# Turned order of the block products in each batch's first pair, 13 instead of 24 loads of w versions, and a new instruction order

## The chip, the cores and the metric

The kernel runs on one core of a Trainium2 chip, as one launch. The metric is device time in microseconds. Three runs of the kernel before gave 339.51, 339.52 and 339.85 us, so its median is 339.52 us. A separate, profiled execution took 343.12 us.

## The reference

Inputs are q, k, v (4 batches, 4 heads, 1088 positions, 32 channels), S1 and S2 (8 x 32), and the weights of a gated layer. Everything is float32.

```
phi(x)  = outer product of (S1 x) and (S2 x), 64 features per position and head
x       = (phi(q) . sum_s phi(k) v) / (phi(q) . sum_s phi(k) + 1e-6)      # [4, 1088, 128]
h       = gelu(x @ w_in)                                                 # d_ff = 1024
u, v    = h[..., :512], h[..., 512:]
v_n     = (v - mean) / sqrt(var + 1e-6) * g_ln
v_s     = einsum('ts,bsd->btd', w_sg, v_n) + b_sg[t]                     # 1088 x 1088 per batch
out     = x + (u * v_s) @ w_out
```

The large product is `w_sg` (called w here) with v_n, once per batch. Most of the work is in it.

## The kernel before, in words

**Precision.** Operands are split in two words, a high one and a low one (`w_h`, `w_l`; the two halves of `ar` for v_n), and a product is three matmuls: high x high, low x high, high x low. These are lines 832, 833 and 834, in `group`.

**Tiling.** The 1088 columns of w (positions t) are three thirds of 362, 362 and 364 columns (`CH`). The 1088 rows are eight tiles of 128 and a last one of 64. The 512 channels of v_n are four blocks of 128. A block of channels times a third of w over all rows is a `whole`: eight groups and a `tail` (lines 843, 844). Results gather in two PSUM banks, `pz0` and `pz1`, which `pair` calls X and Z.

**Seven products instead of eight.** In batches 1 to 3, two blocks of channels (A1 and A2) make a pair, with two pairs in a batch. The first two thirds of w, cut into rows 0 to 511 and 512 to 1023, are treated as a 2 x 2 block matrix, and a pair takes seven block products (`product`, four groups each) of sums of blocks, in place of eight, and two wholes for the third third (results `ca` and `cb`). Sums and differences of v_n blocks are made by VectorE into `tmp` (called `sg`) and into v_n's own place, and split by `words` or `split` into four buffers `ar`; `e` says which buffer a product reads. `evac` (line 763, VectorE) moves a result out of its bank with scale and bias; `unit` makes u (lines 747 to 749), `gate` multiplies the two and adds the product with w_out (lines 784 to 786).

**Versions of w's middle third.** The products need sums of w's blocks. `combine` makes them once, during batch 0, in eight halves one after another: each loads pieces of w into `tmp` (line 880), works on VectorE and ScalarE, and stores the results to a DRAM tensor `td` (lines 897 to 899). One set (`t4`) stays on chip. Four others are in DRAM: "1" and "2" for rows 0 to 511 (half 0), "3" and "b" for rows 512 to 1023 (half 4); "b" is the original. `stream(n, half)` loads one of them over the middle third of `w_h` and `w_l`: two transfers of 362 KB (line 904) and four of 181 KB (line 906), each after the last matmul that reads what it overwrites. `product(..., (0, 1), ...)` and `product(..., (4, 1), ...)` read the streamed versions of half 0 and half 4; `(0, 0)` and `(4, 0)` read the first third, which never changes, and "t4" the set on chip.

**How a pair goes.** In the kernel before each of the six pairs loads all four versions. Its first product of a streamed version comes after one product and a whole. Loads of a pair: "1" after its third product, "b" after its fifth, "2" and "3" further on. Two more loads (lines 1224 and 1225) come ahead of the first pair. The last pair skips "2" and "3".

**Order.** Each operation is a task with a number, given in the order of the program text, and `ORDER` (line 42) lists all 2038 tasks in the order in which they are issued. Each engine, and the queue on SyncE that issues the DMAs, takes its own tasks in that order. Attention of batch b+1 (lines 909 on) is interleaved with the pairs of batch b. Twelve matmuls called `keep` (line 695) compute nothing that is used. At the start, normalisation of batch 0 leads by VectorE (lines 289 to 304, 652, 660) to the first matmuls of w (line 683).

Of the kernel before, what the change touches and what calls it, by code (L numbers as in the profile page):

```python
# [19 lines left out]
NT = 9  # L20
# [174 lines left out]
def tile_kernel(ctx: ExitStack, tc: tile.TileContext, qd, kd, vd, sd, wd, bd, wind, gd, woutd, identd, outd):  # L195
# [142 lines left out]
    g = Gate(0, xs[0])  # L338
# [702 lines left out]
    def pair(b, p, e, zi):  # L1041
# [52 lines left out]
        if more:  # L1094
            stream("2", 0)
# [7 lines left out]
        if more:  # L1103
            stream("3", 4)
# [193 lines left out]
```

## Time and profile before

| | us |
|---|---|
| median of 3 runs | 339.52 |
| profiled execution | 343.12 |
| its span, first to last instruction | 341.3 |
| TensorE matmul (PE) busy | 331.2 |
| TensorE weight loads (PEld) busy | 321.3 |
| VectorE (DVE) busy | 267.0 |
| ScalarE (ACT) busy | 217.9 |
| moved by DMA | 68.87 MB |

Busy times are of one engine over the whole span. Matmuls overlap in the records: a matmul of 362 columns has a row of 0.33 us, but the next starts 0.165 us after it. So the pace is read from the distance of two starts, and not from a row's duration.

### The profile page before, as it was taken

The page shows a single profiled execution, that of the slowest core. Times are in us where ns is not written, and L with a number is a line of the kernel's source. Part 1 is how long each engine was busy: PE and PEld are TensorE (multiplying, and loading weights), DVE is VectorE, ACT ScalarE, POOL GpSimd, SP SyncE. Part 2 cuts the span into 40 slices and gives each one's busy share as a digit, 9 for nine tenths or more (in the row PEclk, how much of TensorE's full clock was granted, in tenths as well). Part 3 has the DMA queues.
Part 4 walks back from the last instruction along what each step waited for, and adds up shares of the span by engine and source line. Part 5 has one row for each costly group of instructions (what it writes and reads, how often), then busy time and mean ns, then how long its engine had stood idle before and what let it go on. Part 6 is the DMA issues. An engine that isn't in the chain of part 4 may idle for free.

```text
span 341.3 us, 5976 instructions
## 1 busy us (share of the span) xinstructions
PE 331.2 (97%) x2000; PEld 321.3 (94%) x2000; DVE 267.0 (78%) x603; ACT 217.9 (64%) x533; POOL 53.1 (16%) x123
## 2 busy tenths in 40 slices
PE   8999999999999999979999999999999999999995
PEld 7996899999999999979999999999989999999994
DVE  3699889999987598858987488988775696767683
ACT  7478882475998976525688895663798873332331
POOL 2595681000004030000000240000003300000000
PEclk9999999999999999989999999999999999999999
DMA  7969554685656476993958855862939474974901
GB/s 236 388 228 346 178 152 106 214 238 129 176 160 181 128 230 180 293 297 100 292 185 268 251 174 187 235 187 82 285 115 314 136 241 120 271 250 131 293 29 67
DMA packets 56175, 68.87 MB, mean 202 GB/s; under 512 B 5008, under 2 KB 53456, under 8 KB 56144
## 3 DMA queue, kind: packets, MB, share of 16 engines
q1 hardware_dynamic: 56000, 68.40, 65.5%
q8 instruction: 16, 0.26, 0.3%
q14 instruction: 15, 0.12, 0.1%
q10 hardware_dynamic: 144, 0.09, 0.1%
HBM read 59.48 MB, written 8.99 MB: 201 GB/s over the span
## 4 chain that ended last, share of the span: by engine, by line
PE 81%; DMA 6%; DVE 6%; ACT 3%; SPq 1%; issue 1%; POOL 0%; DVEq 0%; ACTq 0%
PE pz L832 15%; PE pz L834 15%; PE pz L833 15%; PE ps L930 3%; DMA w_h<-td 2%; PE ps L747 2%; PE ps L748 2%; PE ps L749 2%; PE pz L844 2%; PE pz L843 2%; PE po L786 2%; PE po L785 2%; PE po L784 2%; PE ps L1012 2%; PE ps L1013 2%; PE ps L1014 2%
## 5 line engine op out<-in xcount | busy, mean ns | idle before, releaser
L832 PE MATMUL pz<-w_h,ar 128*128 128x362 f32 (+1 forms) x288 | 96.5, 335 | 2.2 <-DMA w_h<-td 2.2
L834 PE MATMUL pz<-w_l,ar 128*128 128x362 f32 (+1 forms) x288 | 95.3, 331 | 0.0
L833 PE MATMUL pz<-w_h,ar 128*128 128x362 f32 (+1 forms) x288 | 95.1, 330 | 0.0
L832 PEld LDWEIGHTS pz<-w_h,ar 128*128 128x128 f32 x288 | 54.7, 190 | 3.2 <-issue 2.5
L833 PEld LDWEIGHTS pz<-w_h,ar 128*128 128x128 f32 x288 | 54.7, 190 | 0.4
L834 PEld LDWEIGHTS pz<-w_l,ar 128*128 128x128 f32 x288 | 54.6, 190 | 0.3 <-DMA w_l<-td 0.3
L778 ACT CAST gh<-gt 128x362 fp32r<-128x362 f32 (+1 forms) x47 | 22.9, 493 | 24.1 <-PE po L785 12.8
L807 ACT CAST ar<-vn 128x512 fp32r<-128x512 f32 x40 | 24.5, 618 | 20.2 <-PE pz L834 19.4
L309 POOL TENSOR_TENSOR st<-st 128x4 f32<-128x4 f32 (+2 forms) x8 | 2.9, 366 | 190.2 <-DVE st L291 190.2
L779 DVE TENSOR_TENSOR gl<-gt,gh 128x362 fp32r<-128x362 f32 (+1 forms) x47 | 24.6, 529 | 7.9 <-ACT gh L778 7.8
L808 DVE TENSOR_TENSOR ar<-vn,ar 128x512 fp32r<-128x512 f32 x40 | 27.1, 684 | 3.4 <-ACT ar L807 3.1
L753 ACT ACTIVATE u<-ps 128x362 f32<-128x362 f32 (+1 forms) x48 | 21.8, 468 | 9.3 <-PE ps L749 5.9
L326 ACT ACTIVATE vn<-vn,st 128x512 f32<-128x512 f32 x33 | 25.8, 812 | 0.8 <-POOL st L320 0.8
L777 DVE TENSOR_TENSOR gt<-gt,u 128x362 f32<-128x362 f32 (+1 forms) x47 | 24.6, 529 | 0.6
L763 DVE SCALAR_TENSOR_TENSOR gt<-pz,g_col,b_bc 128x362 f32<-128x362 f32 (+1 forms) x31 | 18.3, 590 | 7.5 <-PE pz L834 3.6
L701 POOL TENSOR_TENSOR w_l<-w_f,w_h 128x362 fp32r<-128x362 f32 (+1 forms) x21 | 21.7, 1061 | 5.0 <-ACT w_h L654 4.1
L1021 ACT ACTIVATE vn<-ps 128x512 f32<-128x512 f32 x27 | 16.0, 594 | 5.8 <-PE ps L1014 5.7
L1024 ACT ACTIVATE kp<-vn,st 128x512 bf16<-128x512 f32 x27 | 19.4, 719 | 0.3
L747 PE MATMUL ps<-x_h,win_h 128*128 128x362 f32 (+1 forms) x48 | 15.9, 332 | 0.4 <-ACT ab L958 0.4
L263 DVE TENSOR_TENSOR kp<-ps,kb 128x256 f32<-128x256 f32 x27 | 11.0, 417 | 6.3 <-ACT kb L925 4.5
L784 PE MATMUL po<-gh,wout_h 128*128 128x362 f32 (+1 forms) x47 | 15.8, 337 | 0.0
L748 PE MATMUL ps<-x_h,win_l 128*128 128x362 f32 (+1 forms) x48 | 15.8, 328 | 0.0
(300 smaller groups left out, 813.7 us busy)
## 6 DMA issues: line engine op xcount, KB each, us to landing
w_h<-td SPq DMA_DIRECT2D x48, 362.0 KB
w_l<-td SPq DMA_DIRECT2D x96, 181.0 KB
w_f<-in_w SPq DMA_DIRECT2D x9, 544.0 KB
tmp<-in_w SPq DMA_DIRECT2D x16, 181.0 KB
vx<-in_v SPq DMA_DIRECT2D x8, 288.0 KB
ea<-dq SPq DMA_DIRECT2D x12, 182.0 KB
eb<-dq SPq DMA_DIRECT2D x12, 182.0 KB
td<-tmp SPq DMA_DIRECT2D x8, 271.5 KB
```

The costliest lines, as they stand in the source:

```text
L326: A.activation(self.vn(t), self.vn(t), AF.Identity, bias=self.nm[:, t : t + 1], scale=self.rs[:, t : t + 1])
L747: mm(o, lhsT=win_h[:, ws], rhs=xh[:, cs], start=True, stop=False)
L748: mm(o, lhsT=win_l[:, ws], rhs=xh[:, cs], start=False, stop=False)
L777: add("V", dv(cw), lambda: V.tensor_mul(gt(k)[:, :cw], gt(k)[:, :cw], utt[plan.got[u]][:, :cw]), r=[u], w=[k], free=[u], port=1)
L778: add("A", ac(cw), lambda: A.copy(ght[plan.got[h]][:, :cw], gt(k)[:, :cw]), r=[k], take={h: "gh"})
L779: add("V", dv(cw), lambda: V.tensor_sub(glt[plan.got[l]][:, :cw], gt(k)[:, :cw], f32(ght[plan.got[h]][:, :cw])), r=[h, k], take={l: "gl"}, ...
L784: mm(o, lhsT=wout_h[:, db], rhs=hh, start=i == 1, stop=False, skip_group_check=True)
L807: add("A", ac(n), lambda: A.copy(dst[:, 0], q()), r=r, w=[key])
L808: add("V", dv(n), lambda: V.tensor_sub(dst[:, 1], q(), f32(dst[:, 0])), r=r, w=[key], port=1)
L832: mm(o, lhsT=ar[e][:, 0, t], rhs=wh, start=first, stop=False, skip_group_check=True)
L833: mm(o, lhsT=ar[e][:, 1, t], rhs=wh, start=False, stop=False, skip_group_check=True)
L834: mm(o, lhsT=ar[e][:, 0, t], rhs=wl, start=False, stop=last, skip_group_check=True)
```

## The change

The first pair of each batch (`turn`) takes its products in another order, and the second pair's order is changed a little, so that each pair ends with the versions of half 0 and half 4 that the next one starts with. A first pair uses "1" and "b" and then loads "2" and "3"; a second pair uses "2" and "3" and then loads "1" and "b". That makes two loads per pair, and one ("1") ahead of the first pair: 13 loads in place of 24. Number and shape of the matmuls, of the splits and of VectorE's sums stay as they were. In batch 1 the first pair's first product now reads "1", which is loaded just ahead of it. `ORDER` is a new list of 1972 tasks (66 fewer: 11 loads of six transfers). Three waits (`after=`) are added to the list's own dependencies; they constrain the list and add no instruction.

```diff
-        kw["after"] = gone(b)
+        kw["after"] = [*gone(b), ids["b"], ids["g"], *([ids["ng"]] if col is ng_col else [])]
-            add("PE", 0.222, k1, ..., after=[ids["pv0", NT - 1]] * (b == 1))
+            add("PE", 0.222, k1, ..., after=[ids["pv0", NT - 1], ids["skl"]])
-    def pair(b, p, e, zi):
+    def pair(b, p, e, zi, turn):
...
+        if turn:
+            add_(sg, a[1, 0], a[1, 1], ak[1, 0] + ak[1, 1], gk)
+            words(ar[e[0]], lambda: sg, ("ar", e[0]), gk)
+            split(b, A1, 0, e[1])
+            split(b, A1, 1, e[2])
...
+        if turn:
+            unit(b, ca)
+            product(Z, zk, e[0], (0, 1), True, (1, 1))
+            stream("2", 0)
+            words(ar[e[0]], lambda: sg, ("ar", e[0]), gk)
+            evac(b, c22, Z, zk, g_col)
+            whole(X, xk, 2, (e[1], e[2]), 0)
+            evac(b, ca, X, xk, g_col)
+            gate(b, ca)
+            unit(b, c12)
+            product(Z, zk, e[3], (4, 1), False, (1, 3))
+            stream("3", 4)
+            words(ar[e[3]], lambda: a[0, 0], ("ar", e[3]), ak[0, 0])
+            evac(b, c12, Z, zk, ng_col)
+            unit(b, c11)
+            product(X, xk, e[1], (0, 0), True)
+            split(b, A2, 1, e[1])
+            evac(b, c11, X, xk, g_col)
+            product(Z, zk, e[2], (4, 0), True, (0, 0))
+            split(b, A2, 0, e[2])
+            evac(b, c11, Z, zk, g_col, ("gt", b, c11), False)
+            gate(b, c11)
+            product(X, xk, e[0], (0, 1), False)
+            evac(b, c12, X, xk, g_col, ("gt", b, c12), False)
+            gate(b, c12)
+            unit(b, c22)
+            product(X, xk, e[3], (4, 1), False)
+            evac(b, c22, X, xk, ng_col, ("gt", b, c22), False)
+            gate(b, c22)
+            unit(b, cb)
+            whole(Z, zk, 2, (e[2], e[1]), 1)
+            evac(b, cb, Z, zk, g_col)
+            gate(b, cb)
+            unit(b, c21)
+            product(X, xk, e[1], "t4", False, (0, 2))
+            evac(b, c21, X, xk, ng_col)
+            gate(b, c21)
+            return
+
+        unit(b, c11)
         product(X, xk, e[0], (0, 0), True)
         evac(b, c11, X, xk, g_col)
-        whole(Z, zk, 2, e, 0)
...
+        product(Z, zk, e[1], (4, 0), True, (0, 0))
+        evac(b, c11, Z, zk, g_col, ("gt", b, c11), False)
+        gate(b, c11)
         product(X, xk, e[2], (0, 1), False)
         stream("1", 0)
         split(b, A2, 1, e[2])
         evac(b, c12, X, xk, g_col)
-        product(Z, zk, e[1], (4, 0), True, (0, 0))
+        unit(b, ca)
+        whole(Z, zk, 2, e, 0)
...
         product(X, xk, e[3], (4, 1), False)
         stream("b", 4)
...
         product(Z, zk, e[0], (0, 1), True, (1, 1))
-        if more:
-            stream("2", 0)
...
         product(Z, zk, e[1], (4, 1), False, (1, 3))
-        if more:
-            stream("3", 4)
...
         if ci == 1:
-            stream("2", 0)
-            stream("3", 4)
-    zi, e = 0, (2, 3, 0, 1)
+            stream("1", 0)
+    zi, e = 1, (2, 3, 0, 1)
...
-        pair(b, 0, e, zi)
+        pair(b, 0, e, zi, True)
...
-        pair(b, 1, e, 1 - zi)
+        zi, e = 1 - zi, (e[0], e[3], e[2], e[1])
+        pair(b, 1, e, zi, False)
+        e = (e[0], e[1], e[3], e[2])
```

Up to the first load (task 771) both lists number the tasks alike, so places can be compared. The last stores of `combine` (tasks 717 to 719) stand at places 905 to 917 in the old list and at 860 to 870 in the new one. Of the loads ahead of the first pair, the last transfer of 362 KB (task 774) stands at place 919 in the old list and 896 in the new one; the four groups of the first product that reads it stand at 937 to 944 (tasks 864 to 867) in the old list and at 899 to 924 (tasks 835 to 838) in the new one. The load of k of batch 1 for attention, and its first matmuls (line 922), come after the last `keep` in the new list, and among them in the old one. In batch 1, five groups of the whole on Z stand in the new list between the sixth product of the first pair and the seventh, which use the same bank X.

## Rows read from the trace of the kernel before

**Rows 1.** The page's first part: busy us, share and instructions of each engine.
```profile
PE 331.2 (97%) x2000; PEld 321.3 (94%) x2000; DVE 267.0 (78%) x603; ACT 217.9 (64%) x533; POOL 53.1 (16%) x123
```
**Rows 2.** Stretches of 8 us: busy us and instructions, TensorE's granted clock, DMA.
```profile
core 0: us, PE busy (x) PEld busy (x) DVE busy (x) ACT busy (x) POOL busy (x), PEclk, DMA share, GB/s
24.00:32.00 8.00, 7.98 (x44) 6.29 (x44) 7.20 (x28) 5.71 (x10) 4.64 (x6) 1.00 0.97 342
32.00:40.00 8.00, 7.27 (x43) 6.18 (x41) 7.14 (x20) 6.93 (x24) 6.09 (x16) 1.00 0.80 261
40.00:48.00 8.00, 7.43 (x50) 7.11 (x50) 7.60 (x21) 6.76 (x16) 6.20 (x15) 1.00 0.42 101
64.00:72.00 8.00, 7.58 (x46) 7.28 (x45) 7.32 (x16) 4.53 (x10) 0.00 (x0) 1.00 0.71 185
136.00:144.00 8.00, 8.00 (x48) 7.49 (x47) 6.75 (x14) 4.42 (x9) 0.00 (x0) 1.00 0.92 273
144.00:152.00 8.00, 5.79 (x31) 5.52 (x30) 4.37 (x10) 2.30 (x5) 0.00 (x0) 0.89 1.03 311
152.00:160.00 8.00, 8.00 (x45) 8.00 (x44) 6.48 (x12) 3.81 (x8) 0.00 (x0) 0.89 0.42 120
248.00:256.00 8.00, 7.78 (x43) 7.08 (x42) 5.92 (x14) 7.34 (x24) 0.00 (x0) 1.00 0.34 99
336.00:344.00 8.00, 1.40 (x6) 0.60 (x4) 1.45 (x5) 0.00 (x0) 0.00 (x0) 0.88 0.07 23
```
**Rows 3.** Waits of PE: line waited for, us in total, times, longest.
```profile
PE pz L832 <- DMA w_h<-td: 2.2, 1, 2.2
PE ps L922 <- DMA vn<-in_k: 0.7, 1, 0.7
PE ps L747 <- ACT ab L958: 0.4, 1, 0.4
PE ps L953 <- DVE kp L263: 0.3, 1, 0.3
PE ps L922 <- DVE kp L263: 0.3, 1, 0.3
PE ps L1012 <- ACT vn L1021: 0.2, 1, 0.2
```
**Rows 4.** Timeline 138 to 160: start us, us, engine, line, instruction, idle before.
```profile
138.67 0.33 PE L832 MATMUL pz<-w_h,ar 128*128 128x362 f32 x1
...
140.65 0.19 PEld L834 LDWEIGHTS pz<-w_l,ar 128*128 128x128 f32 x1 [0.28 <-DMA w_l<-td]
...
143.00 0.19 PEld L832 LDWEIGHTS pz<-w_h,ar 128*128 128x128 f32 x1 [0.23 <-DMA w_h<-td]
...
146.78 0.33 PE L833 MATMUL pz<-t4b,ar 128*128 128x362 f32 x1
...
146.95 0.33 PE L834 MATMUL pz<-t4b,ar 128*128 128x362 f32 x1
...
149.48 0.41 PE L832 MATMUL pz<-w_h,ar 128*128 128x362 f32 x1 [2.21 <-DMA w_h<-td]
...
150.44 0.50 PE L832 MATMUL pz<-w_h,ar 128*128 128x362 f32 x1
...
153.74 0.33 PE L832 MATMUL pz<-w_h,ar 128*128 128x364 f32 x1
```
**Rows 5.** The chain that ended last, in order of time: start us, us, what.
```profile
141.22 8.13 DMA w_h<-td
```
**Rows 6.** Timeline of the DMA queue on SyncE, 128 to 152.
```profile
132.06 0.38 SPq L897 DMA_DIRECT2D td<-tmp  x1
...
134.85 0.43 SPq L904 DMA_DIRECT2D w_h<-td  x1
136.77 0.80 SPq L906 DMA_DIRECT2D w_l<-td  x2
```
**Rows 7.** DMA issues by kind, with count and KB of each.
```profile
w_h<-td SPq DMA_DIRECT2D x48, 362.0 KB
w_l<-td SPq DMA_DIRECT2D x96, 181.0 KB
```
**Rows 8.** Groups of VectorE instructions, the results moved out of a bank.
```profile
L763 DVE SCALAR_TENSOR_TENSOR gt<-pz,ng_col,gt 128x362 f32<-128x362 f32 x6 | 3.5, 591 | 2.3 <-PE pz L844 2.2
```

More of the change, by code (lines that the diff above doesn't have):

```diff
@@ L922, in k1 @@
                 mm(ps(pk)[:, :P], lhsT=vn[:, t, 256 * s : 256 * s + P], rhs=sk, start=True, stop=True)
-            add("PE", 0.222, k1, r=[("vn", s, t, 0)], take={pk: "ps"}, tune=at(b, "k", t), after=[ids["pv0", NT - 1]] * (b == 1))
+            add("PE", 0.222, k1, r=[("vn", s, t, 0)], take={pk: "ps"}, tune=at(b, "k", t), after=[ids["pv0", NT - 1], ids["skl"]])
             add("A", 0.09, lambda t=t, pk=pk: A.copy(kbt[t % 2], ps(pk)[:, 32:64]), r=[pk], w=[("kb", t % 2)])
@@ L955, in q2 @@
                 mm(o, lhsT=sk_h, rhs=ql, start=False, stop=True)
-            add("PE", 3 * pe(cw), q2, r=["qh", "ql"], take={pab: "ps"}, tune=at(b, "q", ci), after=[ids["pv0", NT - 1]] * (b == 1))
+            add("PE", 3 * pe(cw), q2, r=["qh", "ql"], take={pab: "ps"}, tune=at(b, "q", ci), after=[ids["pv0", NT - 1], ids["skl"]])
             add("A", ap(cw), lambda cw=cw, pab=pab: A.copy(abt[:, :cw], ps(pab)[:64, :cw]), r=[pab], w=["ab"], free=[pab])
@@ L1051, in pair @@
         end = b == B - 1 and p == 1
-        more = not end
         def both(i, src, r):
@@ L1056, in both @@
             add("V", dv(256), port=1, f=lambda: V.tensor_sub(rs[64:, i : i + 2], src[64:], f32(rs[64:, i : i + 2])), r=r, w=[("rs", i), ("rs", i + 1)])
-        split(b, A1, 0, e[0])
-        split(b, A1, 1, e[1])
-        both(0, vn[:, 8, 256 * s : 256 * s + 256].rearrange("p (t d) -> p t d", d=P), ak[0, 2] + ak[1, 2])
-        add("V", dv(512), port=1, f=lambda: V.tensor_add(a[0, 0], a[0, 0], a[1, 0]), r=ak[1, 0], w=ak[0, 0])
-        add("V", dv(512), port=1, f=lambda: V.tensor_add(sg, a[0, 0], a[1, 1]), r=ak[0, 0] + ak[1, 1], w=gk)
-        words(ar[e[2]], lambda: sg, ("ar", e[2]), gk)
-        words(ar[e[3]], lambda: a[0, 0], ("ar", e[3]), ak[0, 0])
+        add_ = lambda out, x, y, r, w: add("V", dv(512), port=1, f=lambda: V.tensor_add(out, x, y), r=r, w=w)
+        if turn:
[3 more added lines that the diff above has]
+            split(b, A1, 1, e[2])
+        else:
+            split(b, A1, 0, e[0])
+            split(b, A1, 1, e[1])
+        both(0, vn[:, 8, 256 * s : 256 * s + 256].rearrange("p (t d) -> p t d", d=P), ak[0, 2] + ak[1, 2])
+        add_(a[0, 0], a[0, 0], a[1, 0], ak[1, 0], ak[0, 0])
+        add_(sg, a[0, 0], a[1, 1], ak[0, 0] + ak[1, 1], gk)
+        if not turn:
+            words(ar[e[2]], lambda: sg, ("ar", e[2]), gk)
+            words(ar[e[3]], lambda: a[0, 0], ("ar", e[3]), ak[0, 0])
         add("V", dv(512), port=1, f=lambda: V.scalar_tensor_tensor(a[0, 1], sg, -1.0, a[0, 1], op0=ALU.mult, op1=ALU.subtract), r=gk, w=ak[0, 1])
-        add("V", dv(512), port=1, f=lambda: V.tensor_add(sg, a[1, 0], a[1, 1]), r=ak[1, 0] + ak[1, 1], w=gk)
+        if turn:
+            words(ar[e[3]], lambda: a[0, 1], ("ar", e[3]), ak[0, 1])
+        else:
+            add_(sg, a[1, 0], a[1, 1], ak[1, 0] + ak[1, 1], gk)
         add("V", dv(P), port=1, f=lambda: V.tensor_scalar(raw[:, 0], a[1, 2], -1.0, None, op0=ALU.mult), r=ak[1, 2], w=rk)
@@ L1069, in pair @@
         both(2, raw, rk)
-        unit(b, ca)
+        if turn:
+            unit(b, ca)
[9 more added lines that the diff above has]
+            stream("3", 4)
+            words(ar[e[3]], lambda: a[0, 0], ("ar", e[3]), ak[0, 0])
+            evac(b, c12, Z, zk, ng_col)
[24 more added lines that the diff above has]
+        unit(b, c11)
         product(X, xk, e[0], (0, 0), True)
         evac(b, c11, X, xk, g_col)
-        whole(Z, zk, 2, e, 0)
-        evac(b, ca, Z, zk, g_col)
-        gate(b, ca)
-        words(ar[e[0]], lambda: sg, ("ar", e[0]), gk)
-        unit(b, c11)
+        product(Z, zk, e[1], (4, 0), True, (0, 0))
+        evac(b, c11, Z, zk, g_col, ("gt", b, c11), False)
+        gate(b, c11)
         product(X, xk, e[2], (0, 1), False)
@@ L1082, in pair @@
         evac(b, c12, X, xk, g_col)
-        product(Z, zk, e[1], (4, 0), True, (0, 0))
+        unit(b, ca)
+        whole(Z, zk, 2, e, 0)
+        words(ar[e[0]], lambda: sg, ("ar", e[0]), gk)
         words(ar[e[1]], lambda: a[0, 1], ("ar", e[1]), ak[0, 1])
-        evac(b, c11, Z, zk, g_col, ("gt", b, c11), False)
-        gate(b, c11)
-        unit(b, c22)
+        evac(b, ca, Z, zk, g_col)
+        gate(b, ca)
         product(X, xk, e[3], (4, 1), False)
@@ L1091, in pair @@
         evac(b, c22, X, xk, ng_col)
-        unit(b, c21)
+        unit(b, c22)
         product(Z, zk, e[0], (0, 1), True, (1, 1))
-        if more:
-            stream("2", 0)
         evac(b, c22, Z, zk, g_col, ("gt", b, c22), False)
         gate(b, c22)
-        unit(b, c12)
+        unit(b, c21)
         product(X, xk, e[2], "t4", False, (0, 2))
@@ L1101, in pair @@
         gate(b, c21)
+        unit(b, c12)
         product(Z, zk, e[1], (4, 1), False, (1, 3))
-        if more:
-            stream("3", 4)
         evac(b, c12, Z, zk, ng_col, ("gt", b, c12), False)
@@ L1162, in standard @@
         gate(b, (db, ci))
-    add("A", 0.1, lambda: A.mul(ng_col, g_col, -1.0), w=["ng"], after=[ids["g"]])
+    ids["ng"] = add("A", 0.1, lambda: A.mul(ng_col, g_col, -1.0), w=["ng"], after=[ids["g"]])
     def new_swaps():
```

168 rows, old and new, of the table ORDER are left out of this document.

## The prediction

> **What bounds the kernel now.** First the page's busy times: PE is busy 331.2 us of a span of 341.3 us, DVE 267.0, ACT 217.9 [rows 1]. The change keeps all 2000 matmuls, so it can only work on the 10.1 us in which PE is not busy, and on matmuls that run slow. Next the table by stretches says where those 10.1 us lie: 0.73 us in 32 to 40, 0.57 in 40 to 48, 0.42 in 64 to 72, 2.21 in 144 to 152, 0.22 in 248 to 256, and 3.9 at the end, where 1.40 of the last 5.3 us are busy [rows 2]. The end is the last additions and stores, which the change leaves alone. So 144 to 152 is the stretch to look at: PE does 31 matmuls there against 48 in the stretch before, DMA is at a share of 1.03, and this stretch and the next show a granted clock of 0.89 on average where the others show 1.00 [rows 2]. PE's waits name the cause, 2.2 us in line 832 for a transfer of `w_h` from `td`, once [rows 3]. The chain that ended last holds that transfer: issued at 141.22, it took 8.13 us [rows 5]. It belongs to version "1" of the first pair of batch 1.
>
> A rule of the Trainium skill gives another size of the room. Perfetto Trace Analysis, section Identifying the Most-Contended Engine, says that matmul busy time judges TensorE badly and that the busy share of weight loads is to be taken; by that 341.3 - 321.3 = 20.0 us would be open [rows 1], twice as much. The stretch 24 to 32 speaks against it here: weight loads are busy 6.29 us of 8 while PE is busy 7.98 [rows 2], so there a weight load idles behind wide matmuls and nothing can be won.
>
> **The change part by part.**
>
> *Loads removed.* 11 loads go, each of 2 x 362 and 4 x 181 KB [rows 7], 1448 KB: 15.9 MB of 68.87 MB. Nearly all of it is hidden behind PE, which waits for such a transfer once for long and twice for short. What the bunch costs is this. From the start at 146.95 to the next at 149.48 are 2.53 us where the pace is 0.165, so 2.37 us are lost. Then from 150.44 to 153.74 eleven matmuls start, 0.30 us apart where 0.165 is the pace: the clock is at its lower level, 1.2 of 2.4 GHz, after TensorE had stood still, and 3.30 - 11 x 0.165 = 1.48 us are lost. Two short waits of 0.28 and 0.23 us for the same kind of transfer stand before [rows 4]. Together 2.37 + 1.48 + 0.51 = 4.36 us.
>
> Does this go? A group is three matmuls, a product 12, with tail 14, a whole 26. In the kernel before, "1" is loaded after the third product and read by the sixth, with 14 + 12 matmuls between, 4.3 us by the pace, beside units, gates and attention. In the new second pair the whole lies there, and 26 + 12 make 6.3 us. In the new first pair "2" has 26 + 14 + 12 + 14 = 66 matmuls, 10.9 us, and "3" 12 + 14 + 12 = 38, 6.3 us; "b" keeps 14 + 12, 4.3 us. A transfer in the bunch took 8.13 us; one of 181 KB issued at 136.77 and waited for until 140.65 took 3.9 [rows 4, 6]. With two loads in a pair and not four, I take durations near 3.9, so all are covered, and the 4.36 us go. Bounds: all of it goes, or none of it, if the same wait comes back.
>
> *Issue on SyncE.* The 66 DMAs that go free its queue of 66 x 0.43 us [rows 6]; nothing on PE's path waited for the issue alone. I count 0.
>
> *Products turned, one bank twice.* The sixth and the seventh product of a first pair use X one after the other, so the move out of the bank, 0.59 us [rows 8], stands between them unless other work does. In batch 1 five groups on Z do, 15 matmuls or 2.5 us, and the whole offers the same in batches 2 and 3. It costs 0, or without cover 3 x 0.59 = 1.8 us; a gain is excluded, since the matmuls stay the same. I take 0.
>
> *Splits and sums.* Their number is the same (eight splits and four operations of sums per pair), and DVE and ACT have room after 144 [rows 2]: 0.
>
> *New order.* The wait for k of batch 1, 0.7 us [rows 3], should go: its first matmuls now follow the last `keep`, and these twelve cover it. The other waits there, 0.4 + 0.3 + 0.3 + 0.2 = 1.2 us [rows 3], belong to orders that are replaced by others; I see no side, so 0, with bounds of 1.2 us less and 1.2 us more.
>
> *Added dependencies.* They bind the list alone: 0.
>
> **Sum.** 4.36 + 0.7 = 5.06 us, so 343.12 - 5.06 = 338.06 us in the profiled execution (span 336.2, and 1.8 around it as before). How that stands to the median is the weak point. The shown runs have 339.52, 3.6 us less than the profiled one. Without the 4.36 us the profiled one would have 338.76, only 0.76 below the median. So I read the shown runs as the same kernel with most of that stall absent, because transfers there go a little quicker, and not as runs that are 3.6 us quicker everywhere. Then the new kernel has about the same time in both: **338.1 us**, 0.4% less than 339.52.
>
> **The rivals.**
>
> *A: the shown runs hold the whole stall.* Then the 5.06 us come off the median: 334.5 us. For it: the bytes are the same with and without a profile, and DMA is at its limit from 136 to 152, with shares of 0.92 and 1.03 [rows 2]. Against it: it needs 3.6 us of difference spread over a kernel that is 97% matmul.
>
> *B: hidden anyway.* Traffic falls by 23%, but it is beside PE nearly everywhere; if the shown runs have no stall at all and the new order's waits come to as much as the old ones', the time is 339.4 us, no change that can be told. For it: after 160 PE waits for no version at all in the old order. Against it: the 0.7 us wait has a cover now.
>
> *C: a wait takes the place of the one removed.* In the old first pair of batch 1, 12 + 26 + 14 = 52 matmuls needed no streamed version and could stand ahead of the first that does, at 138.67 [rows 4]. In the turned order it is the whole and the product of the first third, 26 + 12 = 38, because the bank Z must begin with the streamed product. PE arrives 14 x 0.165 = 2.3 us earlier, at 136.4, and reaches the fourth group 1.5 us later, at 137.9. The version comes from the last stores of `combine`: one issued at 132.06, the load at 134.85, one transfer of the lead-in still waited for until 140.65 [rows 4, 6]. If `combine` ends when it does now, PE waits 140.65 - 137.9 = 2.75 us, and if the clock falls as before 1.48 more: 338.06 + 4.2 = 342.3 us, slower than before; it decides from some 2.1 us on. For it: the new list has the last load and the product that reads it close together (places 896 and 921). Against it: the new list puts the last stores some 45 places earlier, and by 341.3 / 2038 us for each place this is 7.5 us, more than PE gains; and six transfers are in the lead-in, not twelve.
>
> The Trainium skill would make C smaller: DMA: Bandwidth & Descriptors, section Anatomy of one DMA, gives about 2.0 us and the bytes at 436 GB/s for one transfer (GpSimd's path; here SyncE issues). For 181 KB that is an estimate of 2.4 us and not 3.9, the load would be there at 139.2, the wait 1.3 us, and the time near 339.4, no change. The rows of this stretch, 3.9 and 8.13 us [rows 5, 6], are longer, and I go by them.
>
> **How the numbers follow.** Faster or slower by 0.2%, 0.68 us, is about what can be told. My forecast has 0.50, with 336.9 to 339.3 by the 1.2 us of the order; 0.46 of that is below 338.84 and 0.04 within 0.2%. A has 0.14, faster; B 0.18, same; C 0.18, slower. That gives 0.60, 0.22, 0.18. The range goes from 335.0, which leaves out the end of A (0.05), to 341.5, which leaves out C at its full price (0.08).
>
> **What would show it.** Right: in the new profile no wait of line 832 or 834 for `w_h` or `w_l` over 0.5 us, a granted clock of 1.00 from 16 us to the last stretch, 26 transfers of 362 KB and 52 of 181 KB, PE busy within 1 us of 331, no wait of line 922 for k. Each wait that stays refutes its step by its size. Wrong as a whole: a wait ahead of the first streamed product of batch 1 (C), a median near the old one with all waits gone (B), or a profiled execution again 3 us or more above the median without a stall to explain it (A).

## The result

The changed kernel took 334.84 us (median of 13 runs, 334.02 to 338.45), the kernel before 339.74 us beside it (13 runs, 337.89 to 343.28): a ratio of 0.9876, 95% interval 0.9845 to 0.9908. The forecast was 338.1 us, so the direction was right and the gain was three times the one forecast; the time lies 0.16 us below the range. As a ratio on the 339.52 us that the forecast started from, it would be 335.3 us, just inside the range. Eleven of the 13 runs lie between 334.02 and 335.56 us and two at 338.4; none of these two has a trace, so their cause stays open. The profiled execution took 335.34 us, with a span of 333.2; the median and the profiled time now lie 0.5 us apart, where they were 3.6 us apart before.

In the code behind the change every line between the end of `ORDER` and `pair` has a number lower by two: `group` is L830 to L832, `tail` L841 and L842.

First the page's busy times, as [rows 1]:

```profile
PE 326.9 (98%) x2000; PEld 319.2 (96%) x2000; DVE 264.8 (79%) x603; ACT 219.4 (66%) x533; POOL 54.0 (16%) x123
```

The same 2000 matmuls are now 4.3 us less busy: a matmul that starts late or runs at the lower clock had been counted as busy. Next the stretches of 8 us, as [rows 2] (busy us and instructions of each engine, granted clock, DMA share, GB/s):

```profile
core 0: us, PE busy (x) PEld busy (x) DVE busy (x) ACT busy (x) POOL busy (x), PEclk, DMA share, GB/s
24.00:32.00 8.00, 8.00 (x43) 6.78 (x43) 7.38 (x27) 6.07 (x11) 3.97 (x6) 1.00 0.99 320
32.00:40.00 8.00, 8.00 (x50) 6.80 (x49) 7.72 (x24) 7.49 (x25) 6.33 (x16) 1.00 0.64 193
40.00:48.00 8.00, 8.00 (x59) 8.00 (x58) 6.78 (x18) 5.71 (x16) 7.02 (x15) 1.00 0.37 117
64.00:72.00 8.00, 8.00 (x50) 8.00 (x49) 7.24 (x19) 5.18 (x14) 0.00 (x0) 1.00 0.65 186
136.00:144.00 8.00, 8.00 (x50) 8.00 (x50) 7.23 (x14) 3.75 (x8) 0.00 (x0) 1.00 0.81 271
144.00:152.00 8.00, 8.00 (x49) 7.87 (x48) 7.37 (x16) 4.62 (x10) 0.00 (x0) 1.00 0.82 210
152.00:160.00 8.00, 8.00 (x46) 7.60 (x45) 7.36 (x13) 5.34 (x14) 0.00 (x0) 1.00 0.15 47
248.00:256.00 8.00, 8.00 (x49) 7.86 (x48) 4.60 (x11) 7.39 (x21) 4.50 (x14) 1.00 0.60 207
328.00:336.00 8.00, 1.55 (x7) 0.74 (x5) 1.61 (x5) 0.00 (x0) 0.00 (x0) 0.87 0.08 25
```

The stretch with the stall has PE busy throughout at a clock of 1.00. Two things besides stand in these rows: PE starts 50 and 59 matmuls from 32 to 48 us, where it started 43 and 50, and 50 where it started 46 from 64 to 72 (not all of them the same matmuls, since the order differs). These are not stretches of the version loads.

PE's waits, as [rows 3] (line, us in total, times, longest). Nothing of [rows 3] is left; what is left lies at the start:

```profile
PE pz L515 <- DMA vx<-in_v: 1.7, 2, 1.5
PE ps L256 <- POOL vx L218: 0.9, 1, 0.9
```

The chain of work that ended last, by engine, before:

```profile
PE 81%; DMA 6%; DVE 6%; ACT 3%; SPq 1%; issue 1%; POOL 0%; DVEq 0%; ACTq 0%
```

and after:

```profile
PE 96%; DMA 1%; SPq 1%; DVE 1%; issue 0%; DVEq 0%
```

The issues of the loads, as [rows 7], now with the median us from issue to landing at the end of each row:

```profile
w_l<-td SPq DMA_DIRECT2D x52, 181.0 KB, 4.6
w_h<-td SPq DMA_DIRECT2D x26, 362.0 KB, 4.4
```

The profile's total is 52.54 MB, 16.3 MB less than before. (The prediction's 15.9 MB is the same amount, with 1024 bytes to a KB and 1000 KB to a MB.)

**Where the time went.** Waits under 0.2 us and late starts inside busy time don't show in the views above. So for every matmul I took the distance from its start to the next start, less the usual distance for that number of columns (the lower quartile of the same trace), and added up what is left by stretch, in us. The 0.9 us ahead of the first start are left out. The usual distances add up to 320.6 us in all of these, so the rows below are the whole difference; only in e1 they are 321.3 us, so that 0.7 us of its time stand in no row.

| us lost | before | e0 (before again) | e1 (fewer bytes) | after | e5 (after again) | e4 (old head) |
|---|---|---|---|---|---|---|
| 0 to 24 | 3.79 | 3.26 | 3.96 | 3.51 | 3.48 | 3.66 |
| 24 to 48 | 2.70 | 2.55 | 2.47 | 0.96 | 0.98 | 2.58 |
| 48 to 72 | 0.90 | 0.75 | 0.44 | 0.13 | 0.13 | 0.88 |
| 72 to 136 | 0.76 | 0.84 | 1.12 | 0.74 | 0.75 | 0.72 |
| 136 to 160 | 4.61 | 1.58 | 0.17 | 0.22 | 0.23 | 0.23 |
| 160 to 240 | 0.99 | 0.96 | 0.77 | 0.96 | 0.94 | 0.95 |
| 240 to 256 | 0.65 | 0.64 | 0.63 | 0.19 | 0.19 | 0.21 |
| 256 to the last start | 1.30 | 2.16 | 0.91 | 1.13 | 1.16 | 1.17 |
| behind the last start | 4.12 | 3.84 | 3.76 | 3.88 | 3.69 | 3.89 |
| sum | 19.82 | 16.59 | 14.22 | 11.70 | 11.54 | 14.28 |

From before to after, 4.39 us of 8.1 are the stretch of the stall, and 2.51 lie between 24 and 72 us.

### The profile page after: what moved, and what is told of

Its sections match the earlier page's. It is cut to its first block, busy times and chain, and to the rows that moved or that the text cites. A ratio compares the mean times of both kernels' runs of the same rounds, so it can differ in the third digit from the quotient of the medians.

```text
span 333.2 us, 5905 instructions
## 1 busy us (share of the span) xinstructions
PE 326.9 (98%) x2000; PEld 319.2 (96%) x2000; DVE 264.8 (79%) x603; ACT 219.4 (66%) x533; POOL 54.0 (16%) x123
## 2 busy tenths in 40 slices
DMA packets 43854, 52.54 MB, mean 158 GB/s; under 512 B 3952, under 2 KB 41136, under 8 KB 43824
## 3 DMA queue, kind: packets, MB, share of 16 engines
HBM read 43.17 MB, written 8.99 MB: 157 GB/s over the span
## 4 chain that ended last, share of the span: by engine, by line
PE 96%; DMA 1%; SPq 1%; DVE 1%; issue 0%; DVEq 0%
PE pz L830 16%; PE pz L832 16%; PE pz L831 15%; PE ps L928 4%; PE ps L747 2%; PE ps L746 2%; PE ps L745 2%; PE po L784 2%; PE po L783 2%; PE po L782 2%; PE pz L842 2%; PE pz L841 2%; PE ps L1010 2%; PE ps L920 2%; PE ps L1011 2%; PE ps L1012 2%
## 5 line engine op out<-in xcount | busy, mean ns | idle before, releaser
L830 PE MATMUL pz<-w_h,ar 128*128 128x362 f32 (+1 forms) x288 | 95.6, 332 | 0.0
L832 PE MATMUL pz<-w_l,ar 128*128 128x362 f32 (+1 forms) x288 | 94.6, 328 | 0.0
L830 PEld LDWEIGHTS pz<-w_h,ar 128*128 128x128 f32 x288 | 54.2, 188 | 0.7
L832 PEld LDWEIGHTS pz<-w_l,ar 128*128 128x128 f32 x288 | 54.2, 188 | 0.0
L1022 ACT ACTIVATE kp<-vn,st 128x512 bf16<-128x512 f32 x27 | 19.4, 718 | 0.2
L782 PE MATMUL po<-gh,wout_h 128*128 128x362 f32 (+1 forms) x47 | 15.9, 339 | 0.0
L745 PE MATMUL ps<-x_h,win_h 128*128 128x362 f32 (+1 forms) x48 | 15.9, 331 | 0.0
L747 PE MATMUL ps<-x_l,win_h 128*128 128x362 f32 (+1 forms) x48 | 15.8, 329 | 0.0
```

Source lines behind the costliest of these rows:

```text
L745: mm(o, lhsT=win_h[:, ws], rhs=xh[:, cs], start=True, stop=False)
L782: mm(o, lhsT=wout_h[:, db], rhs=hh, start=i == 1, stop=False, skip_group_check=True)
L830: mm(o, lhsT=ar[e][:, 0, t], rhs=wh, start=first, stop=False, skip_group_check=True)
L832: mm(o, lhsT=ar[e][:, 0, t], rhs=wl, start=False, stop=last, skip_group_check=True)
```

## The experiments

Theory L: the gain is the version loads (bytes and bunches). Theory O: a good part of it is the searched order, in stretches that have nothing to do with those loads. Kernels of one group ran on the same chip and share the runs of the kernel before.

**First group: the bytes, and the head of the list.** The kernel before ran beside these with a median of 341.35 us (28 runs, 337.9 to 345.75).

*e0_before_again*: the kernel before with no edit, as one more kernel of the group.

> The kernel before, unchanged, to see span and clock of each of its runs. If the shown runs lack most of the 4.4 us stall of the profiled one (the forecast's reading), most runs have a clock of 1.00 and lie at 338 to 339 us, and only those near 341 to 343 us have a clock of 0.995. If they hold it (rival A), most have a clock near 0.995 whatever their time. Ratio to the kernel before 1.000 in both cases.

340.17 us (12 runs, 338.36 to 341.91), ratio 0.9969 (0.9938 to 1.0). Its profiled execution took 340.0 us. PE's waits there for versions, and the stretch of the stall, as in [rows 2, 3]:

```profile
PE pz L832 <- DMA w_h<-td: 1.6, 2, 1.1
```
```profile
144.00:152.00 8.00, 6.90 (x42) 6.62 (x41) 5.16 (x11) 2.86 (x6) 0.00 (x0) 1.00 1.07 310
```

The stall is there in an execution of ordinary length too, but shorter: 1.58 us are lost from 136 to 160 and not 4.61, and the clock stays at 1.00. Of e0's 12 runs one has a mean clock of 0.995 and the other 11 have 0.997 or more, so the long stall with its slow clock is the exception, as the forecast had it and against rival A; but the runs lie at 338.4 to 341.9 us and not at the 338 to 339 us expected. So the shown runs, which have no trace, probably held part of the stall. The ratio says one thing more: two measurements of one kernel differ by 0.3% here.

*e1_fewer_bytes*: the kernel before, the same loads at the same places, each of 196 columns instead of 362 (some 13 loads' worth of bytes).

```diff
-load(f32(w_h[:, half + t : half + t + 2, 362:724]), TD[n][t : t + 2, 0].rearrange(by))
+load(f32(w_h[:, half + t : half + t + 2, 362:558]), TD[n][t : t + 2, 0, :, :196].rearrange(by))
-load(f32(w_l[half + t][:, 362:724]), TD[n][t, 1])
+load(f32(w_l[half + t][:, 362:558]), TD[n][t, 1, :, :196])
```

> The kernel before with its old list and all 24 loads, each loading 196 of 362 columns: the bytes of 13 full loads, the same count of transfers (the output is not the reference's, since the other columns keep an older version). Theory L (the gain is the traffic): the wait of 2.2 us for w_h and the slow clock behind it go, the profile shows some 338.8 us, and the ratio to the kernel before is 0.988 to 0.993. Theory O (the gain is the new list, the loads hardly matter): ratio 0.997 to 1.000, and waits for w_h or w_l stay near 2 us.

338.33 us (11 runs, 337.32 to 339.88), ratio 0.9915 (0.9886 to 0.9945). No product waits for a version any more; what waits from 24 to 72 us is nearly as before (the 0.4 us of L747 in [rows 3] are not among it):

```profile
PE ps L922 <- DMA vn<-in_k: 0.4, 1, 0.4
PE ps L922 <- DVE kp L263: 0.3, 1, 0.3
PE ps L953 <- DVE kp L263: 0.3, 1, 0.3
```
```profile
32.00:40.00 8.00, 7.50 (x44) 6.23 (x42) 7.30 (x20) 7.09 (x24) 6.10 (x16) 1.00 0.76 249
40.00:48.00 8.00, 7.45 (x50) 7.26 (x51) 7.60 (x21) 6.95 (x16) 6.42 (x15) 1.00 0.41 104
144.00:152.00 8.00, 8.00 (x50) 8.00 (x49) 7.13 (x15) 4.41 (x9) 0.00 (x0) 1.00 0.75 210
```

So fewer bytes are worth 1.84 us against e0 (3.0 against the median of all runs of before in this group), and with them the stall is gone: 0.17 us are lost from 136 to 160, and 0.27 and 0.23 us in e8 and e9 below, which load as little. What they leave unexplained is some 3 us by the medians and by the spans of the profiled executions (336.5 and 333.2 us). By the ratios to before (0.9915 here, 0.9876 and 0.9846 for the changed kernel) it is 1.3 to 2.3 us, and the intervals overlap. So L alone probably doesn't suffice; the second group tests this on one chip.

*e2_traffic_back*: the changed kernel, 11 of its 13 loads made twice, the second time to a place in DRAM that nobody reads.

```diff
+def twice(dst, src, copy):
+    load(dst, src)
+    if more:
+        load(copy, src)
```

> The new kernel with 11 of its 13 loads made twice, the second time to a place in DRAM that nothing reads: traffic and count of transfers as before the change, list and products as after it. Theory L: waits for w_h or w_l of 1 to 4 us come back in the pairs, ratio to the kernel before 0.995 to 1.000. Theory O: 0.986 to 0.990 as for the new kernel, and no such wait over 0.5 us.

345.06 us (6 runs, 343.03 to 345.93), ratio 1.0106 (1.0062 to 1.015), some 10 us more than the changed kernel.

```profile
PE pz L832 <- DMA w_l<-td: 3.0, 3, 1.2
PE pz L830 <- DMA w_h<-td: 3.0, 2, 2.1
```
```profile
152.00:160.00 8.00, 5.86 (x25) 5.28 (x24) 6.22 (x15) 4.45 (x11) 0.00 (x0) 0.79 0.95 262
```

The waits for versions and the lower clock are back: 6.05 us are lost from 136 to 160 (0.22 in the changed kernel) and 4.67 from 256 to the last start (1.13), but 0.95 from 24 to 48, as in the changed kernel. The ratio lies above the ranges of both theories, and the size proves less than it seems: the old loads wrote on chip and these copies write to DRAM, where the profile counts 25.31 MB written and not 8.99. That the new order doesn't hide 16.3 MB more of this traffic is shown; what 24 real loads would cost in it stays open.

*e3_new_head*: the kernel before with the first 354 places of its list (some 55 us) in the new order and the others as they were.

```diff
 ORDER = [
-    0, 10, 11, 12, 13, 14, 15, 16, 17, 41, 42, 1, 47, 50, 44, 49, 43, 46, 48, 45, 53, 77, 78, 54,
+    0, 1, 2, 10, 3, 4, 5, 6, 7, 11, 12, 13, 14, 15, 16, 17, 47, 8, 48, 49, 44, 45, 41, 42,
...
```

> The kernel before with the first 354 places of its list (up to some 58 us) in the order of the new list, the rest in the old order. By the trace the start, 24 to 48 us, lost 2.7 us of PE in the old kernel and 1.0 in the new one. Theory O: 1.7 us go, ratio to the kernel before 0.993 to 0.996. Theory L: the later stall sets the end whatever the start does, since its transfers begin when combine ends: ratio 0.998 to 1.001, and the wait in 144 to 152 grows by what the start saves.

340.14 us (12 runs, 338.15 to 341.56), ratio 0.9972 (0.994 to 1.0003): the same as e0. From 24 to 48 us only 0.95 us are lost, but from 64 to 72 us 2.14, with the wait of the second row below, which neither kernel has. The first row is the stall; from 136 to 160 us 2.13 us are lost, 0.55 more than in e0.

```profile
PE pz L832 <- DMA w_h<-td: 1.6, 1, 1.6
PE ps L979 <- ACT u L753: 1.1, 1, 1.1
```
```profile
64.00:72.00 8.00, 6.68 (x38) 5.83 (x37) 7.88 (x18) 4.85 (x11) 0.00 (x0) 1.00 0.61 175
```

By itself this speaks against O, or the cut makes a wait of its own. The second group does it the other way round.

**Second group: the changed kernel, one thing undone.** Before beside them: 340.16 us (16 runs, 338.54 to 342.87).

*e5_after_again*: no edit.

> The changed kernel unchanged, as the reference for the other three on one chip. Theory L (the lost time of the kernel before hung on the 24 large loads and their bunches, and on the old order of the first 60 us): 334.8 us, 0.9876 of the kernel before, within 0.3% of the first measurement. Theory V (most of the first measurement's gain was a kernel before that happened to stall in those runs): 337.5 to 338.5 us, a ratio of 0.993 or more.

335.27 us (6 runs, 334.5 to 336.02), ratio 0.9846 (0.9805 to 0.9886). The gain holds on another chip than that of the first group, and its losses by stretch are those of the first profile within 0.1 us but for the end (0.19). V falls.

*e4_old_head*: the first 354 places, as many as in e3, in the old order. Its diff is that of e3 with the two first lines exchanged.

> The changed kernel, its list's places of the first 58 us put back in the order of the list before. Theory O (the searched order is what removed 1.7 us from 24 to 48 us and 0.7 us from 64 to 72 us): 336.5 to 337.3 us, and TensorE's waits of 24 to 48 us come back to about 2.7 us. Theory L (those waits went because the queues carry less): 334.8 us as the changed kernel, with less than 1 us lost from 24 to 48 us.

337.88 us (11 runs, 337.12 to 338.63), ratio 0.992 (0.9892 to 0.9948): 2.6 us more than e5, and the two ranges of runs don't touch. The waits are again those of the kernel before or of their kind, with the loads untouched:

```profile
PE ps L920 <- ACT w_h L652: 0.7, 1, 0.7
PE ps L978 <- DVE kvl L940: 0.4, 1, 0.4
PE ps L951 <- DVE kp L261: 0.3, 1, 0.3
PE ps L920 <- DVE kp L261: 0.3, 1, 0.3
```
```profile
32.00:40.00 8.00, 7.26 (x43) 6.04 (x41) 7.23 (x20) 7.02 (x24) 6.11 (x16) 1.00 0.78 254
40.00:48.00 8.00, 7.53 (x50) 7.34 (x51) 7.60 (x21) 6.73 (x17) 6.22 (x15) 1.00 0.38 108
144.00:152.00 8.00, 8.00 (x51) 8.00 (x50) 7.51 (x15) 3.71 (x9) 0.00 (x0) 1.00 0.67 180
```

43 and 50 matmuls, as in [rows 2]. This is what O said, 0.6 us above its upper end, and the third row shows that the stall's stretch has no part in it.

*e6_after_fewer_bytes*: the changed kernel's 13 loads cut to 106 of 362 columns, as in e1.

> The changed kernel with its 13 remaining loads cut to 106 of 362 columns, so that part of the products takes stale columns. Theory 'the stall is used up' (no product waits for these loads any more): the time of the changed kernel, 334.8 us, within 0.5 us. Theory 'traffic goes on costing' (each byte on the queues delays something, as the 1.8 to 3.0 us that 24 smaller loads gave in the kernel before): 333.0 to 334.0 us, and the spread between runs shrinks.

335.38 us (6 runs, 334.49 to 335.96), against 335.27 of e5: no difference that can be told. What e1 gave in the old kernel is used up; the 13 loads that stay are hidden.

*e7_v_ahead*: the first two loads of v issued ahead of the second and third of q, to remove the largest wait that is left.

```diff
-        yield "q1", (0.5,), lambda: load_q(1)
-        yield "q2", (0.45, 0.18), lambda: load_q(2)
...
+        yield "q1", (0.5,), lambda: load_q(1)
+        yield "q2", (0.45, 0.18), lambda: load_q(2)
```

> The changed kernel with the first two loads of v issued ahead of the second and third of q on SyncE's queue. The product that begins the first state waits 1.5 to 1.7 us for them at 7 to 9 us. Theory 'the load is late' : the wait falls to nothing, 333.3 to 334.0 us. Theory 'something else is as late' (q's own products or the weights behind them wait in its place): 334.8 us or up to 1.5 us more, with a wait for q's load in the list of waits.

335.03 us (6 runs, 334.48 to 335.33): the same as e5. The wait for the load is gone, and others stand in its place, for VectorE and not for q's load:

```profile
PE pz L515 <- DVE vn L261: 0.9, 2, 0.6
PE pz L557 <- DVE sg_kvx L527: 0.7, 1, 0.7
```

No version of these beats the changed kernel by more than can be told.

**Third group: do the two parts add?** Before beside them: 339.6 us (19 runs, 338.27 to 344.22).

*e8_bytes_head*: the kernel before with both edits, e1's and e3's. *e9_bytes_head43*: the same with 306 places (some 48 us) in the new order and not 354.

> The kernel before with both halves of the change imitated at once: its 24 loads of versions cut to 196 of 362 columns (part of the products takes stale columns), and the first 354 places of its list (some 55 us) in the new order. Theory S (the two gains are of separate places and add: 1.8 us by the bytes, 2.6 us by the head): 335.7 us, a ratio near 0.984, and no wait of over 0.5 us between 24 and 160 us. Theory G (the old list behind the cut gives the head's gain back, as it did with all bytes): 338.0 to 338.6 us, with a wait of 1 us or more for ScalarE at 64 to 72 us.

> As the one before, but only the first 306 places (some 48 us) in the new order. Theory S: 335.7 to 336.5 us, since the stretch from 24 to 48 us, where 2.5 us went, is still covered. Theory G: 338.0 to 338.6 us; if the give-back at 64 to 72 us comes only from where the cut lies, it is smaller here than with 354 places.

e8: 337.86 us (12 runs, 336.96 to 338.84), ratio 0.9929 (0.9899 to 0.9959). e9: 337.17 us (8 runs, 336.39 to 337.68), ratio 0.9914 (0.9883 to 0.9945). Neither comes near 335.7. PE's waits from 24 to 72 us in e8 are

```profile
PE ps L979 <- ACT u L753: 1.1, 1, 1.1
```

and in e9

```profile
PE ps L922 <- DMA vn<-in_k: 0.8, 1, 0.8
PE po L685 <- DVE ar L660: 0.5, 1, 0.5
```

e8 loses 1.01 us from 24 to 48 and 1.68 from 64 to 72; e9 2.50 and 0.19. The loss moves with the cut and doesn't go; why e9 loses 2.50 us in a stretch that the new order covers stays open. G fits e8, with its wait for ScalarE, though the time lies 0.14 us below G's range; e9 lies between the two theories. A piece of the new order ahead of the rest of the old one is worth 0.5 to 1.2 us against e1's 338.33, and these ratios can't be told from e1's. Of all lists that were run, only the whole new one has some 3 us.

*e10_old_head24*: the changed kernel with the first 160 places (some 29 us) in the old order.

> The changed kernel with the places of only the first 29 us or so in the order of the list before (58 us of it cost 2.6 us). If TensorE's waits from 24 to 48 us are set by what was put ahead of them: 337 to 338 us with 2 us or more lost from 24 to 48 us. If they are set by the places of that stretch itself: 335.3 us as the changed kernel, with about 1 us lost there.

336.25 us (6 runs, 336.05 to 336.99), ratio 0.9889 (0.9847 to 0.993). Its stretches:

```profile
24.00:32.00 8.00, 7.98 (x42) 6.25 (x42) 6.42 (x24) 6.15 (x11) 4.62 (x7) 1.00 1.03 339
32.00:40.00 8.00, 7.44 (x42) 6.15 (x41) 7.62 (x24) 7.09 (x25) 5.37 (x13) 1.00 0.58 176
40.00:48.00 8.00, 7.96 (x59) 7.77 (x58) 7.39 (x21) 5.39 (x15) 7.10 (x16) 1.00 0.26 74
```

2.35 us are lost from 24 to 48 (0.98 in e5) although nearly all places of that stretch are the new ones: what was put ahead of it sets most of the loss. The time, 336.25 us, lies between the two theories. It is 1.0 us more than e5's by the medians of two groups, with ratios whose intervals overlap; the trace says more than the time here.

**A run for the queue.** Before beside it: 340.76 us (11 runs).

*e11_issues_back*: e2 with 16 of 362 columns in each copy, so that the 66 issues come back and the bytes don't.

```diff
-        load(copy, src)
+        load(copy[..., :16], src[..., :16])
```

> The changed kernel with the 66 removed DMAs put back on SyncE's queue, as a copy that nobody reads, but each with 16 of 362 columns, so that the issues and the pieces come back and the bytes don't (with all bytes it took 345.1 us). Theory 'issue costs nothing' (the prediction's 0, and the bytes make the loss): 335.0 to 336.0 us and no wait of a product for a version. Theory 'queue time counts' (66 x 0.43 us on SyncE put later loads behind): 338 us or more, with waits for loads of versions or of k and v in the list.

336.24 us (6 runs, 336.03 to 338.1), ratio 0.9866 (0.9826 to 0.9907). Just above the first theory's end, and the interval includes the changed kernel's 0.9876. One product waits for a version, briefly:

```profile
PE pz L830 <- DMA w_h<-td: 0.3, 1, 0.3
```

By the medians the issues cost 1.0 us against e5 and 1.4 us against the first measurement, by the ratios between nothing and 0.7 us, and these are other chips: some 1 us, if anything. So nearly all of e2's 10 us are its bytes.

## Why the prediction came out as it did

**Loads: right in size for the execution that I read.** The forecast was 4.36 us; from 136 to 160 us 4.39 went, by the mechanism named: no wait of L830 or L832 for `w_h` or `w_l`, a clock of 1.00 throughout. e1 shows the cause alone: fewer bytes, same places, no stall. That the execution read held a stall nearly three times as long as e0's was chance, so its size doesn't carry over to other runs. One rival was not run: in the old list the transfer that the product waits for, issued at 141.22, stands behind a load of q and two transfers of the same version that are read later. It is the second of the two in the last of these rows of the queue:

```profile
139.73 0.43 SPq L947 DMA_DIRECT2D qld<-in_q  x1
140.37 0.32 SPq L906 DMA_DIRECT2D w_l<-td  x1
140.79 1.05 SPq L904 DMA_DIRECT2D w_h<-td  x2
```

A kernel before with this transfer ahead of the other three could have a shorter stall with all its bytes.

**New order: the step that failed.** I put 0.7 us, for the wait for k, and 0 for the rest, "I see no side", with 1.2 us to either side. The rest of the difference between the two profiled executions is 8.10 - 4.39 = 3.71 us, of which 2.51 lie from 24 to 72 us and 0.46 from 240 to 256. e4 shows 2.6 us of it by putting the head back. The rest is not taken apart: no run separates the turned order of the products from the new list behind its first 354 places. With 3.71 in place of 0.7 the sum gives 338.06 - 3.01 = 335.05 us; 335.34 and 334.84 were measured. (That is no test, since 3.71 is read from the same two executions.) Two things made the term small. I took its bound from the list of waits [rows 3], which holds 1.7 us for 24 to 72 us, where the starts lose 3.6. And I said that the change "can only work on the 10.1 us in which PE is not busy, and on matmuls that run slow": busy time itself held lost time, and it fell by 4.3 us where I expected 1 at most. That sign went against my own sum, too, since the 1.48 us of slow matmuls in it are busy time. Nor is my list of where the 10.1 us lie complete: it adds up to 8.1, and the other 2.0 lie between 0 and 24 us, where the change moved little (3.79 us lost before, 3.51 after).

The Trainium skill was nearer with the room. By the rule of Perfetto Trace Analysis, section Identifying the Most-Contended Engine, 20.0 us were open; by the starts 19.82 us were lost. So close a fit is chance: by the same two counts it is 19.4 and 16.59 us in e0, 14.0 and 11.70 in the changed kernel. I set the rule aside because of one stretch, 24 to 32 us, where 1.71 us of weight-load idle stand beside 0.46 us lost. For that stretch the objection holds, for the sum it doesn't.

**The median.** I read the shown runs as the kernel with "most of that stall absent" and expected about the same new time in the profiled execution and the others. That came true (335.34 and 334.84). Part of the stall was there, though: 1.58 us in e0, and e1's 1.84 us by the medians. So the 4.9 us from e0 to e5 are some 1.8 us of loads and some 3 us that are left for the order, of which e4 shows 2.6.

**Issue 0, bank twice 0, splits 0.** e11 puts the issue at some 1 us at most. From 160 to 240 us, where the turned pair of batch 2 lies, 0.99 us were lost before and 0.96 after, so the bank used twice costs nothing that shows.

**The rivals.** A gave 334.5 us, nearest to the result, by a mechanism that isn't the one: it takes the whole 4.36 us off the median, and e1 gives 1.84. The number fits because the order gives what the loads don't. B is refuted by the time. C did not happen. The last of `combine`'s stores by lines 897 to 899 and the first streamed product of batch 1 moved together. Before, the queue's row of that store is

```profile
133.99 0.33 SPq L899 DMA_DIRECT2D td<-tmp  x1
```

and after (the same line's number is L897)

```profile
125.18 0.33 SPq L897 DMA_DIRECT2D td<-tmp  x1
```

8.8 us earlier, where I had worked out 7.5 from the places. The product that reads the first streamed version began at 138.67 [rows 4] and now begins here, with no wait:

```profile
130.01 0.33 PE L830 MATMUL pz<-w_h,ar 128*128 128x362 f32 x1
```

That is 8.7 us earlier and not the 2.3 us that I had from 14 matmuls: the list moved PE's side as far as the queue's. The loads' 4.4 us (362 KB) and 4.6 us (181 KB) from issue to landing are near the 3.9 that I took. The estimates of 2.85 and 2.4 us by the Trainium skill's formula (DMA: Bandwidth & Descriptors, section Anatomy of one DMA), which is for another path, GpSimd's, are further off.

## What to carry to other kernels

When the whole list of a kernel's work is replaced, its worth need not be bounded by the waits that a profile lists, and here it wasn't: add up the distances between starts by stretch first, for they also hold the small delays and the late starts that busy time covers. A part of the new order had hardly any worth when it was grafted on the rest of the old one (e3, e8, e9); undoing a part of the new order instead (e4, e10) showed where the loss appears. A single profiled execution that is 1% longer than the median may hold a stall that varies from run to run: profile the kernel again before putting that stall's size on the median.

## What was not expected of the hardware

The stall's length varies while the program doesn't: 1.58 us were lost from 136 to 160 in e0 and 4.61 in the first profile, with the same 68.87 MB (whether on the same chip is not on record). After e0's longest wait for a version, 1.1 us, and e3's, 1.6 us, the granted clock stayed at 1.00; after 2.2 us [rows 3] it was 0.89 on average in two stretches, and in e2, after waits of up to 2.1 us, 0.79 in one. So the longest stall cost more than its own length, by the 1.48 us of slow matmuls that the prediction counted. With fewer bytes most groups of runs also draw together: the standard deviation of e0's 12 runs is 1.2 us, that of e1's 11 runs 0.7, that of e5's six 0.6. But the changed kernel's 13 runs in the result, with the two at 338.4 us, have 1.4, so this is not shown for certain.
